# Routing of a fused attention and mixture-of-experts kernel: four chunks of tokens in place of two

## The chip, the cores and the metric

The kernel runs on one core of a Trainium2 chip. What counts is the device time of one execution in microseconds. Five engines work side by side, each through its own queue in order: TensorE (PE; PEld is its weight load), VectorE (DVE), ScalarE (ACT), GpSimd (POOL) and SyncE (SP), which issues most DMAs. Waits between engines are semaphores.

## The reference

Three layers follow each other: attention through 32 packed queries, a mixture of eight experts of which each token takes two, and a feed-forward layer. Cut to what matters here:

```python
p_packed = sm_attn(p, k, v)              # 4 batches, 8 heads, 576 rows, 64 wide
out = sm_attn(q, p_packed, p_packed)     # -> x: 2304 tokens x 512

logits = x @ w_gate                      # 8 experts
noisy_logits = logits + np.log1p(np.exp(x @ w_noise)) * noise
top2 = np.argpartition(-noisy_logits, 2, axis=1)[:, :2]
top2_w = softmax of the two chosen logits
for e in range(E):                       # h: 1024 wide
    out[mask] += top2_w * (np.maximum(x[mask] @ w1[e], 0.0) @ w2[e])

h = x @ w_in                             # 2048 wide
return (h * sigmoid(h)) @ w_out
```

## The kernel before

The 2304 tokens are 18 tiles of 128. Attention works them off in units of two tiles (tiles 8 and 17 alone). Its last phase, `unpacked` (L409), leaves for each tile a row block in DRAM (`xs`, L467) and 16 logits (`lg`, L462 and L464). A loop over 16 slots (L616) writes the attention phases of several units in turn; `START1`, `START2` and the `LAG`s say which phase stands in which slot.

`route` (L470) takes a chunk of n tiles and makes of its logits the row numbers by which tokens are fetched for the experts. It is a generator of eight to ten steps, nearly all on VectorE, each over all n tiles at once:

- noisy logits (rt_w, rt_sa, rt_h, rt_sp, rt_ny; L478 to L493; two steps on ScalarE),
- the two best experts of each token (L497, L499: one instruction a tile; rt_oh, rt_ob),
- a token's rank within its expert: matmuls into `rk` (L510 to L514) that count earlier tokens, those of earlier chunks through `seen_b`,
- rank into slot: rt_rs, rt_sf, rt_hi, rt_hs, rt_lo; then two one-hot tiles, rt_oc (L527, L529) and rt_oa (L534, three tiles a piece), whose product `ip` (L541, 2n matmuls) adds this chunk's tokens to the table of row numbers `idx_f`,
- slots and gates, by which the results are put together again much later (L567 to L581).

Before, there are two chunks. The first, tiles 0 to 10 (`EARLY` = 11), starts when their logits are there. From it comes `idx0`, the first 256 row numbers of expert 0 (L544), with which two gathers on GpSimd (`fetch`, L196) bring the rows of expert 0's first block. Tiles 11 to 17 are the second chunk; it is written within expert 0's first block (L661 to L672), beside its matmuls. When it is done (`idx`, L554), five more gathers bring three tiles for expert 0's second block and two for expert 1, which are transposed on TensorE (`transposed`, L153) and split into a high and a low part by ScalarE and VectorE.

`expert_block` (L235) runs eight steps f: twelve matmuls into `hps` (L208 to L210), relu and split on ScalarE (hh) and VectorE (hl, L232), and one step later the matmuls into `acc` (L218 to L220). The first block of expert 0 has 256 tokens, its second 384.

Up to the end of that first block a scheduler sets the order of each engine's queue by its own estimate of the times; the order in which the code is written is its input. Behind it, `pin` keeps TensorE and ScalarE in written order. The buffers of `rk`, `xp`, `pp`, `ip`, `c` and `i4` are two that go round (pool `pMx`).

Of the kernel before, what the change touches and what calls it, by code (L numbers as in the profile page):

```python
# [7 lines left out]
F32 = mybir.dt.float32  # L8
# [6 lines left out]
OP = mybir.AluOpType  # L15
AX = mybir.AxisListType
# [3 lines left out]
P = 128  # L20
B, H, S, D, PK = 4, 8, 576, 64, 32
N, DM, E, F, FF = 2304, 512, 8, 1024, 2048
NT = N // P
ET = 5
CAP = ET * P
# [5 lines left out]
START2 = (3, 4, 5, 5, 6, 6, 8, 11, 12, 12)  # L31
SWITCH = 12
WLOAD = 4
RSTEP = 3
LAG2 = (0, 1, 3, 3)
# [9 lines left out]
def body(ctx: ExitStack, tc: tile.TileContext, q, k, v, p, wg, wn, noise, w1, w2, w_in, w_out, out):  # L45
# [212 lines left out]
    with ExitStack() as ax:  # L258
# [211 lines left out]
        def route(t0, n, lg):  # L470

            def tl(shape, nm, dt=F32):
                return rt.tile([P, n, *shape], dt, name=f"rt_{nm}{n}", tag=f"rt_{nm}", bufs=1)
# [39 lines left out]
            for j in range(n - 1):  # L513
                T.matmul(rk[:, j + 1:, :], ones, ob[:, j:j + 1, :].to_broadcast([P, n - 1 - j, E]),  # L514
                         start=False, stop=j == n - 2)
            rs = tl([E], "rs")
# [25 lines left out]
            if t0 + n < NT:  # L542
                V.tensor_tensor(idx_f, idx_f, ip, op=OP.add)
                V.tensor_scalar(idx0, idx_f[:, 0:TA], 0.0, float((t0 + n) * P - 1), op0=OP.max, op1=OP.min)  # L544
                sn = rt.tile([P, E], F32, name=f"sn{n}")
                V.tensor_reduce(sn, ob.rearrange("p n e -> p e n"), axis=AX.X, op=OP.add)
                V.tensor_tensor(seen, seen, sn, op=OP.add)
                V.tensor_copy(seen_b, seen)
                c = pMx.tile([P, E], F32, name="c", tag="m")
                T.matmul(c, ones, seen_b, start=True, stop=True)  # L550
                V.tensor_scalar(few, c, float(TA * P), float(N), op0=OP.is_lt, op1=OP.mult)
            else:
                V.tensor_tensor(idx_f, idx_f, ip, op=OP.add)
                V.tensor_scalar(idx, idx_f, 0.0, float(N - 1), op0=OP.max, op1=OP.min)  # L554
                V.tensor_scalar(idx_f, idx_f, 0.0, float(N - 1), op0=OP.max, op1=OP.min)  # L555
                i4 = pMx.tile([P, 4, E * ET], F32, name="i4", tag="m")
                for g in range(4):
                    for a in range(4):
                        T.matmul(i4[32 * a:32 * a + 32, g, :], ident[:, 32 * g:32 * g + 32], idx_f, start=True, stop=True,
                                 tile_position=(0, 32 * a))  # L560
                V.tensor_scalar(idx4, i4, 4.0, quad[:, 0:1], op0=OP.mult, op1=OP.add)
                sn = rt.tile([P, E], F32, name=f"sn{n}")
                V.tensor_reduce(sn, ob.rearrange("p n e -> p e n"), axis=AX.X, op=OP.add)
                V.tensor_tensor(seen_b, seen, sn, op=OP.add)
# [4 lines left out]
            V.scalar_tensor_tensor(rr, ch, -float(CAP), sf, op0=OP.mult, op1=OP.add)  # L569
            V.tensor_scalar(late, rr, split_at - 63.5, None, op0=OP.is_ge)  # L570
            V.tensor_scalar(up, ch, float((TB - TA) * P), float((E - 1) * TA * P), op0=OP.mult, op1=OP.add)
# [5 lines left out]
            V.tensor_tensor(ex, m8[:, :, 1:2], m8[:, :, 0:1], op=OP.subtract)  # L577
# [6 lines left out]
        chunks = {0: EARLY, EARLY: NT - EARLY}  # L584
# [24 lines left out]
        def run(gen, n):  # L609
            for _ in range(n):  # L610
                next(gen, None)

        r0 = route(0, EARLY, lgs[0])
        W[0] = []
        M["delay"] = 2
        for slot in range(START2[-1] + LAG2[-1] + 1):  # L616
# [30 lines left out]
            if slot >= START2[5] + LAG2[3]:  # L647
                run(r0, RSTEP)
        for _ in r0:
            pass  # L650
        tick()
        tick()
        r1 = route(EARLY, NT - EARLY, lgs[EARLY])
# [7 lines left out]
        for f in expert_block(0, 0, TA, X["a"]):  # L661
            run(r1, 2)
            if f == 4:
                for _ in r1:
                    pass
# [290 lines left out]
```

## Time and profile before

| | us |
|---|---|
| time, median of 3 runs | 995.01 (994.36 to 996.98) |
| the profiled execution | 991.13 |
| its span in the profile | 989.30 |
| TensorE busy | 957.0 (97%) |
| VectorE busy | 447.4 (45%) |
| ScalarE busy | 346.4 (35%) |
| GpSimd busy | 313.4 (32%) |

The profile is one execution; 1.83 us of it lie outside the span. Attention and routing fill the first 118 us, expert 0's first block runs to 149 us, the other experts and the last layer fill the rest. The 97% of TensorE is a mean over stretches with different limits: a kernel of this kind is read by stretch.

### The profile page before, as it was taken

Reading aid. Unit: us, or ns where it says so; the run is one execution under the profiler, and the core shown is the slowest. Engines: PE = TensorE matmul, PEld = TensorE weight load, DVE = VectorE, ACT = ScalarE, POOL = GpSimd, SP = SyncE. Lnnn points to the kernel's source line nnn. Section 1 sums busy time; section 2 is a strip of 40 time slices with the busy share of each in tenths; the row PEclk is TensorE's granted clock in tenths of the full one; section 3 lists DMA queues with packets and bytes.
Section 4 is the critical chain, followed back from the end, with each engine's and each line's share of the span. In section 5 each row is a group of like instructions: output and inputs, shape, how many; then the busy total and the mean of one; then the engine's idle time right before and its main releaser. Section 6 shows DMA issues by size and latency. Waiting matters only on the chain.

```text
span 989.3 us, 14385 instructions
## 1 busy us (share of the span) xinstructions
PE 957.0 (97%) x5584; PEld 821.0 (83%) x5584; DVE 447.4 (45%) x871; ACT 346.4 (35%) x631; POOL 313.4 (32%) x345
## 2 busy tenths in 40 slices
PE   6989799999999999999999999999999999999996
PEld 4767589899999999998999988888888888888884
DVE  4537763666767576766634557222122221111111
ACT  3567322433434343433323343322222222222221
POOL 2166214343525243443200136333323322222221
PEclk9989899999999999999999999999999999999998
DMA  9994324576757676566623454111011110001001
GB/s 243 249 270 161 107 65 125 188 231 202 231 167 227 188 235 199 189 226 207 188 64 117 149 194 136 54 28 37 22 53 33 32 43 1 1 1 43 0 1 46
DMA packets 82298, 122.49 MB, mean 124 GB/s; under 512 B 16432, under 2 KB 49200, under 8 KB 82224
## 3 DMA queue, kind: packets, MB, share of 16 engines
q1 hardware_dynamic: 74704, 101.58, 32.6%
q0 software_dynamic: 7520, 19.93, 7.0%
q8 instruction: 46, 0.75, 0.3%
q14 instruction: 28, 0.23, 0.1%
HBM read 93.17 MB, written 28.31 MB: 123 GB/s over the span
## 4 chain that ended last, share of the span: by engine, by line
PE 90%; DVE 4%; DMA 3%; ACT 1%; SPq 1%; issue 1%; ACTq 0%
PE hps L208 14%; PE hps L210 14%; PE hps L209 14%; PE acc L219 14%; PE acc L218 14%; PE acc L220 14%; PE xp L460 1%; PE tps L157 1%; PE s L429 1%; PE s L362 1%; DMA vm<-in_v_dram 1%; DMA km<-in_k_dram 1%; DVE rt_oa L534 1%; PE kp L351 0%; DMA raw<-wf_out 0%
## 5 line engine op out<-in xcount | busy, mean ns | idle before, releaser
L176 POOL DMA_INDIRECT xg<-xs,idx x120 | 127.0, 1059 | 195.1 <-DVE xturn L185 147.6
L750 POOL TENSOR_TENSOR gl<-sg,gh 128x512 fp32r<-128x512 f32 (+1 forms) x80 | 95.4, 1194 | 253.5 <-ACT gh L749 237.9
L231 ACT ACTIVATE hh<-hps 128x384 fp32r<-128x384 f32 (+1 forms) x128 | 56.0, 438 | 260.5 <-PE hps L210 256.8
L746 DVE TENSOR_TENSOR sg<-hps,sg 128x512 f32<-128x512 f32 (+1 forms) x80 | 50.7, 634 | 196.2 <-ACT sg L745 196.0
L232 DVE SCALAR_TENSOR_TENSOR hl<-hps,hh 128x384 fp32r<-128x384 f32 (+1 forms) x128 | 62.4, 488 | 122.0 <-ACT hh L231 121.3
L745 ACT ACTIVATE sg<-hps 128x512 f32<-128x512 f32 (+1 forms) x80 | 44.2, 553 | 189.5 <-PE hps L210 189.2
L749 ACT ACTIVATE gh<-sg 128x512 fp32r<-128x512 f32 (+1 forms) x80 | 47.1, 589 | 79.3 <-DVE sg L746 79.1
L736 POOL DMA_INDIRECT y<-ys,slots x36 | 36.7, 1019 | 110.9 <-DVE hl L232 72.4
L739 DVE TENSOR_SCALAR y<-y,gates 128x512 f32<-128x512 f32 x18 | 10.9, 607 | 37.9 <-DMA y<-ys,slots 37.9
L740 DVE SCALAR_TENSOR_TENSOR y<-y,gates,y 128x512 f32<-128x512 f32 x18 | 15.7, 871 | 25.1 <-DMA y<-ys,slots 25.0
L460 PE MATMUL xp<-ppBD,a2T 128*128 128x272 f32 (+1 forms) x80 | 23.5, 433 | 1.6 <-ACT xr L51 0.8
L185 DVE STREAM_TRANSPOSE xturn<-xg 128x512 f32<-128x512 f32 x30 | 21.2, 706 | 3.7 <-DMA wf_in<-t 2.5
L689 DVE SCALAR_TENSOR_TENSOR t<-raw,t 128x512 int32<-128x512 int32 x32 | 22.2, 693 | 0.9
L690 DVE SCALAR_TENSOR_TENSOR t<-raw,t 128x512 int32<-128x512 int32 x32 | 22.1, 691 | 0.9
L196 POOL DMA_INDIRECT xg<-xs,idx x10 | 9.7, 969 | 40.3 <-DVE idx_f L555 19.5
L686 ACT ACTIVATE t<-raw 128x512 f32<-128x512 f32 x32 | 21.2, 662 | 0.1
L208 PE MATMUL hps<-xha,wa3h 128*128 128x256 f32 (+1 forms) x56 | 17.7, 316 | 1.8 <-DVE sg L746 1.8
L160 DVE TENSOR_TENSOR xla<-tps,xha 128x512 fp32r<-128x512 f32 x14 | 9.6, 690 | 21.1 <-ACT xha L159 21.1
L53 DVE COPY ysb<-acc 128x512 f32<-128x512 f32 x24 | 16.4, 682 | 4.9 <-PE acc L220 4.8
L429 PE MATMUL s<-ppT,qT 128*128 128x64 f32 x128 | 17.9, 291 | 0.0
L208 PE MATMUL hps<-xha,wa0h 128*128 128x256 f32 (+1 forms) x56 | 17.6, 314 | 0.2 <-ACT xha L159 0.2
L208 PE MATMUL hps<-xha,wa2h 128*128 128x256 f32 (+1 forms) x56 | 17.7, 316 | 0.1
(450 smaller groups left out, 2976.4 us busy)
## 6 DMA issues: line engine op xcount, KB each, us to landing
raw<-in_moe_w_dram SPq DMA_DIRECT2D x56, 512.0 KB, 4.0
ys<-ysb SPq DMA_DIRECT2D x40, 256.0 KB, 3.7
raw<-in_moe_w_in_dram SPq DMA_DIRECT2D x16, 512.0 KB, 4.3
raw<-in_moe_w_out_dram SPq DMA_DIRECT2D x16, 512.0 KB, 4.1
xs<-xr SPq DMA_DIRECT2D x18, 256.0 KB, 2.1
km<-in_k_dram SPq DMA_DIRECT2D x8, 512.0 KB, 7.6
vm<-in_v_dram SPq DMA_DIRECT2D x8, 512.0 KB, 7.6
qm<-in_q_dram SPq DMA_DIRECT2D x8, 512.0 KB, 7.1
```

The source lines that it names most:

```text
L176: G.indirect_dma_start(out=xg[:, g * P:(g + 1) * P], out_offset=None, in_=xs[:, :].rearrange("n (a f) -> (n a) f", a=4), in_offset=bass.In ...
L208: T.matmul(ps, wh[:, c, s], xh[:, c, :n], start=c == 0, stop=False)
L209: T.matmul(ps, wh[:, c, s], xl[:, c, :n], start=False, stop=False)
L210: T.matmul(ps, wl[:, c, s], xh[:, c, :n], start=False, stop=c == 3)
L218: T.matmul(y, hh[:, s], wh[:, f % 2, :], start=f == 0, stop=False)
L219: T.matmul(y, hh[:, s], wl[:, f % 2, :], start=False, stop=False)
L220: T.matmul(y, hl[:, s], wh[:, f % 2, :], start=False, stop=f == last)
L231: A.activation(hh, ps, AF.Relu)
L232: V.scalar_tensor_tensor(hl, ps, 0.0, hh.bitcast(F32), op0=OP.max, op1=OP.subtract)
L746: V.tensor_tensor(sg, ps, sg, op=OP.mult)
L749: A.activation(gh, sg, AF.Copy)
L750: G.tensor_tensor(gl, sg, gh.bitcast(F32), op=OP.subtract)
```

## The change

`route` is called for four chunks, of tiles 0 to 5, 6 to 10, 11 to 14 and 15 to 17. A table, `ROUTE`, says in which slot how many steps of which chunk are written; the steps of the last chunk that are left are written in the first step f of expert 0's block. The routing tiles have two buffers (`bufs=2`) in place of one. The count `seen` is brought up right behind the rank matmuls, `idx0` and `few` are made only after tile 10, and three instructions that begin slots and gates are kept in written order behind the row numbers (`keep_in_program_order`).

```diff
-RSTEP = 3
+ROUTE = {8: ((0, 4),), 9: ((0, 99), (6, 3)), 10: ((6, 99),), 14: ((11, 5),), 15: ((11, 99), (15, 3))}
...
-                return rt.tile([P, n, *shape], dt, name=f"rt_{nm}{n}", tag=f"rt_{nm}", bufs=1)
+                return rt.tile([P, n, *shape], dt, name=f"rt_{nm}{n}", tag=f"rt_{nm}", bufs=2)
...
+            sn = rt.tile([P, E], F32, name=f"sn{t0}", tag="rt_sn", bufs=2)
+            V.tensor_reduce(sn, ob.rearrange("p n e -> p e n"), axis=AX.X, op=OP.add)
+            V.tensor_tensor(seen, seen, sn, op=OP.add)
+            V.tensor_copy(seen_b, seen)
             rs = tl([E], "rs")
...
-                V.tensor_scalar(idx0, idx_f[:, 0:TA], 0.0, float((t0 + n) * P - 1), op0=OP.max, op1=OP.min)
...
+                if t0 + n == EARLY:
+                    V.tensor_scalar(idx0, idx_f[:, 0:TA], 0.0, float((t0 + n) * P - 1), op0=OP.max, op1=OP.min)
+                if t0 + n == EARLY:
+                    c = pMx.tile([P, E], F32, name="c", tag="m")
...
-            V.scalar_tensor_tensor(rr, ch, -float(CAP), sf, op0=OP.mult, op1=OP.add)
+            tc.keep_in_program_order(V.scalar_tensor_tensor(rr, ch, -float(CAP), sf, op0=OP.mult, op1=OP.add))
...
-        chunks = {0: EARLY, EARLY: NT - EARLY}
+        chunks = {0: 6, 6: 5, 11: 4, 15: 3}
...
-            if slot >= START2[5] + LAG2[3]:
-                run(r0, RSTEP)
-        for _ in r0:
-            pass
+            for t, k in ROUTE.get(slot, ()):
+                run(rs[t], k)
...
         for f in expert_block(0, 0, TA, X["a"]):
-            run(r1, 2)
+            run(rs[15], 99)
             if f == 4:
-                for _ in r1:
-                    pass
                 rows = fetch(xs[:, :], idx, TA, TB) + fetch(xs[:, :], idx, ET, TA)
```

How this moves instructions shows at two places. The first is VectorE's queue where attention is at its seventh unit; sd, mx, kT and s are attention's tiles, lg the logits. Before:

```order
L368 TENSOR_REDUCE mx<-s_1139 128x1
L462 TENSOR_TENSOR lg_201<-xp,lg_201 128x16
L369 TENSOR_SCALAR mx<-mx 128x1
L443 TENSOR_REDUCE mx_1046<-sd_1048 128x16
L444 TENSOR_SCALAR mx_1046<-mx_1046 128x16
L445 RECIPROCAL mx_1046<-mx_1046 128x16
```

After:

```order
L369 TENSOR_SCALAR mx<-mx 128x1
L478 TENSOR_TENSOR rt_w_1205<-lg_201 128x48
L479 TENSOR_SCALAR rt_sa_1208<-lg_201 128x48
L483 TENSOR_SCALAR rt_sp_1207<-lg_201 128x48
L482 TENSOR_SCALAR rt_h_1206<-rt_w_1205 128x48
L485 TENSOR_SCALAR rt_big_1209<-rt_w_1205 128x48
L484 TENSOR_TENSOR rt_h_1206<-rt_h_1206,rt_w_1205 128x48
L443 TENSOR_REDUCE mx_1048<-sd_1050 128x16
L487 SCALAR_TENSOR_TENSOR rt_h_1206<-rt_h_1206,rt_w_1205 128x48
L444 TENSOR_SCALAR mx_1048<-mx_1048 128x16
L487 SCALAR_TENSOR_TENSOR rt_h_1206<-rt_h_1206,rt_w_1205 128x48
L445 RECIPROCAL mx_1048<-mx_1048 128x16
```

The first steps of the chunk of six now stand ahead of and between attention's steps, some 12 us earlier in the program than the first steps of the chunk of eleven did.

The second place is TensorE's queue at the end of expert 0's first block (numbers of lines that the change has shifted are those of the changed file). Before, the transposes of the five gathered tiles (tps, four instructions a tile) stand apart: two times 8 ahead of the acc matmuls of f = 5 and f = 6, and the last 4 here, ahead of those of f = 7:

```order
L220 MATMUL acc<-wa7h,hl 128x512 x2
L157 MATMUL tps<-ident,xg 128x128 x4
L218 MATMUL acc<-wa7h,hh 128x512
L219 MATMUL acc<-wa7l,hh 128x512
L218 MATMUL acc<-wa7h,hh 128x512
L219 MATMUL acc<-wa7l,hh 128x512
L220 MATMUL acc<-wa7h,hl 128x512 x2
L208 MATMUL hps<-xhb,wa0h 128x384
```

After (i is idx4's matmul, c the count):

```order
L220 MATMUL acc<-wa7h,hl 128x512 x2
L561 MATMUL i_2027<-idx_f,ident 32x40 x16
L662 LDWEIGHTS ones
L662 MATMUL c<-seen_b,ones 128x8
L218 MATMUL acc<-wa7h,hh 128x512
L219 MATMUL acc<-wa7l,hh 128x512
L218 MATMUL acc<-wa7h,hh 128x512
L219 MATMUL acc<-wa7l,hh 128x512
L220 MATMUL acc<-wa7h,hl 128x512 x2
L157 MATMUL tps<-ident,xg 128x128 x20
L208 MATMUL hps<-xhb,wa0h 128x384
```

All five tiles are now transposed in a row ahead of the second block's first matmul (hps of xhb), and the matmuls of the last ip, which before stood ahead of the fifth of the eight steps f, stand ahead of the hps of the last one; those of i, before behind the fifth hps, stand behind the last.

## Rows read from the trace of the kernel before

**Rows 1.** Busy time by stretch: stretch, length, busy of each engine, PEclk, DMA.
```profile
120.00:150.00 30.00, 29.29 (x232) 24.28 (x231) 18.41 (x85) 8.38 (x21) 4.76 (x5) 1.00 0.22 70
150.00:300.00 150.00, 150.00 (x836) 136.44 (x836) 92.67 (x141) 56.36 (x93) 59.87 (x58) 1.00 0.62 194
```

**Rows 2.** Busy time by stretch, as rows 1: PE, PEld, DVE, ACT, POOL.
```profile
77.00:90.00 13.00, 12.64 (x106) 9.98 (x105) 7.92 (x31) 11.90 (x29) 4.71 (x6) 1.00 0.64 219
90.00:110.00 20.00, 13.23 (x199) 10.43 (x198) 19.63 (x92) 7.17 (x21) 8.71 (x17) 0.89 0.29 94
110.00:118.50 8.50, 7.33 (x42) 4.72 (x39) 4.98 (x14) 4.20 (x11) 3.77 (x4) 0.85 0.40 125
```

**Rows 3.** Timeline of VectorE, tiles 0 to 10: start, duration, instruction.
```profile
89.82 0.25 DVE L478 TENSOR_TENSOR rt_w<-lg 128x88 f32<-128x88 f32 x1
...
109.70 0.17 DVE L544 TENSOR_SCALAR idx<-idx_f 128x2 int32<-128x2 f32 x1
```

**Rows 4.** Timeline of VectorE, tiles 11 to 17.
```profile
122.52 0.22 DVE L478 TENSOR_TENSOR rt_w<-lg 128x56 f32<-128x56 f32 x1
...
128.37 0.41 DVE L232 SCALAR_TENSOR_TENSOR hl<-hps,hh 128x256 fp32r<-128x256 f32 x1
...
134.34 0.18 DVE L554 TENSOR_SCALAR idx<-idx_f 128x40 int32<-128x40 f32 x1
```

**Rows 5.** Timeline of GpSimd's weight splits and of VectorE beside and apart from them.
```profile
76.87 2.78 POOL L119 TENSOR_TENSOR wa5l<-raw,wa5h 128x256 fp32r<-128x256 f32 x4
...
91.14 2.86 POOL L119 TENSOR_TENSOR wa6l<-raw,wa6h 128x256 fp32r<-128x256 f32 x4 [5.03 <-PE pp L388]
91.96 0.77 DVE L487 SCALAR_TENSOR_TENSOR rt_h<-rt_h,rt_w 128x88 f32<-128x88 f32 x1
...
95.14 2.81 POOL L119 TENSOR_TENSOR wa7l<-raw,wa7h 128x256 fp32r<-128x256 f32 x4
97.19 0.17 DVE L577 TENSOR_TENSOR rt_ex<-rt_m 128x11 f32<-128x11 f32 x1
...
123.36 0.22 DVE L487 SCALAR_TENSOR_TENSOR rt_h<-rt_h,rt_w 128x56 f32<-128x56 f32 x1
```

**Rows 6.** Timeline around the gathers (in brackets idle before), and how long they take to land.
```profile
110.79 1.15 POOL L196 DMA_INDIRECT xg<-xs,idx  x1 [6.32 <-PE s L436]
...
133.51 0.55 PE L541 MATMUL ip<-rt_oc,rt_oa 128*128 128x40 f16 x8 [0.55 <-DVE rt_oa L534]
134.79 0.98 POOL L196 DMA_INDIRECT xg<-xs,idx  x1 [19.45 <-DVE idx_f L555]
139.82 0.95 POOL L196 DMA_INDIRECT xg<-xs,idx  x1 [0.30 <-issue]
DMA to landing us min/median/max: 3.5/3.6/3.7
```

**Rows 7.** Timeline of TensorE at the end of expert 0's first block.
```profile
136.26 0.49 PE L559 MATMUL i<-idx_f,ident 128*32 128x40 f32 x32
...
136.72 0.47 PE L218 MATMUL acc<-wa6h,hh 128*128 128x512 f32 x1
...
145.11 0.28 PE L208 MATMUL hps<-xha,wa3h 128*128 128x256 f32 x1
...
147.01 0.60 PE L157 MATMUL tps<-ident,xg 128*128 128x128 f32 x4
...
149.02 0.45 PE L208 MATMUL hps<-xhb,wa0h 128*128 128x384 f32 x1
```

**Rows 8.** TensorE by stretch (length, busy, granted clock, DMA), and one wait.
```profile
54.00:56.00 2.00, 2.00 (x13) 0.64 1.03 322
60.00:62.00 2.00, 2.00 (x46) 0.65 1.09 305
104.00:106.00 2.00, 0.65 (x4) 0.94 0.21 68
104.53 0.65 PE L451 MATMUL a2p<-ident,sd 128*128 128x128 f32 x4 [1.94 <-POOL sd L446]
```

More of the change, by code (lines that the diff above doesn't have):

```diff
@@ L543, in route @@
                 V.tensor_tensor(idx_f, idx_f, ip, op=OP.add)
-                V.tensor_scalar(idx0, idx_f[:, 0:TA], 0.0, float((t0 + n) * P - 1), op0=OP.max, op1=OP.min)
[L545 to L551, printed above, removed]
+                if t0 + n == EARLY:
+                    V.tensor_scalar(idx0, idx_f[:, 0:TA], 0.0, float((t0 + n) * P - 1), op0=OP.max, op1=OP.min)
+                if t0 + n == EARLY:
+                    c = pMx.tile([P, E], F32, name="c", tag="m")
+                    T.matmul(c, ones, seen_b, start=True, stop=True)
+                    V.tensor_scalar(few, c, float(TA * P), float(N), op0=OP.is_lt, op1=OP.mult)
             else:
@@ L561, in route @@
                 V.tensor_scalar(idx4, i4, 4.0, quad[:, 0:1], op0=OP.mult, op1=OP.add)
-                sn = rt.tile([P, E], F32, name=f"sn{n}")
-                V.tensor_reduce(sn, ob.rearrange("p n e -> p e n"), axis=AX.X, op=OP.add)
-                V.tensor_tensor(seen_b, seen, sn, op=OP.add)
             yield
@@ L568, in route @@
             rr, late, up = tl([2], "rr"), tl([2], "late"), tl([2], "up")
-            V.scalar_tensor_tensor(rr, ch, -float(CAP), sf, op0=OP.mult, op1=OP.add)
+            tc.keep_in_program_order(V.scalar_tensor_tensor(rr, ch, -float(CAP), sf, op0=OP.mult, op1=OP.add))
             V.tensor_scalar(late, rr, split_at - 63.5, None, op0=OP.is_ge)
-            V.tensor_scalar(up, ch, float((TB - TA) * P), float((E - 1) * TA * P), op0=OP.mult, op1=OP.add)
+            tc.keep_in_program_order(V.tensor_scalar(up, ch, float((TB - TA) * P), float((E - 1) * TA * P), op0=OP.mult, op1=OP.add))
             V.tensor_tensor(up, up, late, op=OP.mult)
@@ L576, in route @@
             ex, dn = tl([1], "ex"), tl([1], "dn")
-            V.tensor_tensor(ex, m8[:, :, 1:2], m8[:, :, 0:1], op=OP.subtract)
+            tc.keep_in_program_order(V.tensor_tensor(ex, m8[:, :, 1:2], m8[:, :, 0:1], op=OP.subtract))
             A.activation(ex, ex, AF.Exp)
@@ L611, in run @@
                 next(gen, None)
-        r0 = route(0, EARLY, lgs[0])
+        rs = {t: route(t, n, lgs[t]) for t, n in chunks.items()}
         W[0] = []
@@ L646, in body @@
                         load_w2(W[0], 0, i - 4, G)
-            if slot >= START2[5] + LAG2[3]:
-                run(r0, RSTEP)
-        for _ in r0:
-            pass
+            for t, k in ROUTE.get(slot, ()):
+                run(rs[t], k)
         tick()
         tick()
-        r1 = route(EARLY, NT - EARLY, lgs[EARLY])
         for i in "ab":
```

## The prediction

> **What bounds the kernel now.** I read the busy time by stretch first, then TensorE's waits, then VectorE's instructions in order of time in the stretch where TensorE is not full. From 120 us on TensorE is busy nearly without a gap: 29.29 of 30 us, then 150.00 of 150 [rows 1]. So whatever the change does to the moment when the long expert stage begins is passed on whole to the end, and whatever it does to VectorE after that is hidden. What is left to win lies ahead: between 90 and 118.5 us TensorE is busy 20.56 of 28.5 us, 7.9 us idle, while VectorE is busy 19.63 of the first 20 [rows 2]. That is the routing of tiles 0 to 10, from 89.82 us (rt_w) to 109.70 (idx, the first row numbers) [rows 3], with attention's steps for the last tiles queued among it. Between 77 and 90 us it is the other way round: TensorE is busy 12.64 of 13 us, VectorE 7.92, so VectorE has 5.1 us idle there [rows 2].
>
> The second half, tiles 11 to 17, runs on VectorE from 122.52 to 134.52 us [rows 4], beside the first block of expert 0 on TensorE. Its row numbers feed five gathers on GpSimd; their rows must lie in SBUF, transposed, when the second block (hps at 149.02) begins [rows 6, 7]. Today that has much room.
>
> **The change, term 1: the gathers behind the last chunk.** In the order of the changed kernel the last row numbers come far later relative to expert 0's first block. Before, ip of the second half stands ahead of the fifth of the block's eight steps f. Now three tiles have a chunk of their own, whose ip stands just ahead of the last hps (f = 7), and all five transposes, 20 instructions, stand between the block's last matmul and the second block's first. From the end of ip to that hps two things race.
> - The gathers: ip ends at 133.51 + 0.55 = 134.06; idx ends at 134.34 + 0.18 = 134.52, so 0.46; the first gather starts 0.27 later, at 134.79; the fifth at 139.82, so 5.03 more; a gather lands 3.6 us after it starts (3.5 to 3.7) [rows 4, 6]; the last transpose takes 0.44 (four matmuls at the 0.11 pitch of full clock, estimated from the row of four at 147.01, 0.60 long with the pipeline's tail, next start after 0.35 to 0.44) [rows 7]. Sum 0.46 + 0.27 + 5.03 + 3.6 + 0.44 = 9.8 us.
> - TensorE's own work: from the first hps of f = 7 to the second block's hps before, 145.11 to 149.02, 3.9 us with one transposed tile in it; four more tiles at 0.44, 1.8; the matmuls of idx4 and c, 0.46 (136.26 to 136.72) [rows 7]. Sum 6.1 us.
>
> So TensorE idles 9.8 - 6.1 = **3.7 us**, where before it idled nothing (the rows were there). This supposes that VectorE is in time for ip. Laying its steps for tiles 15 to 17 against TensorE's steps f = 4 to 6, I find oa done about 1 us ahead of ip, so the term is 3.6 to 3.8 if that holds, and up to 5.2 if VectorE is 1.5 us later than I think.
>
> **Term 2: the clock behind that stall.** TensorE's granted clock is at 1.2 GHz, half of full, in two stretches. In the first it falls inside 54 to 56 us (mean 0.64) and rises inside 60 to 62 (0.65): 1.4 + 4 + 1.4 = 6.8 us. The second begins just ahead of 106 us (0.94 over 104 to 106), after TensorE had been busy 0.65 us of 2, and had idled 1.94 us ahead of that [rows 8]; 102.6 us, where this idling began, is 3.2 us earlier. The new stall is of that kind: five transposes, 2.2 us of work, in some 6 us. If the clock falls 3.2 us into it and stays down for 6.8, then 6.8 - (5.9 - 3.2) = 4.1 us of dense matmuls run at half speed and cost 2.0 more. No row shows a stall that is 37% busy, so the ends are 0 (it stays up) and 3.4 (it falls as the stall ends: half of 6.8). I take **2.0**.
>
> **Term 3: VectorE from 77 to 110 us.** A chunk has a cost that doesn't depend on its tiles. Eleven tiles take 89.82 to 109.87, 20.05 us; in this lie 14 attention instructions, 4.1 us from start to start, and 2.4 us of slowed instructions (below), so 13.6 us pure [rows 3]. Seven tiles take 122.52 to 134.41, 11.9 us; less three hl steps (0.41 a piece, 0.35 from start to start) and 0.4 of idling, 10.4 us pure [rows 4]. The difference, 3.2 us for four tiles, gives 0.8 us a tile and 4.9 fixed. Two chunks of 6 and 5 instead of one of 11 add 4.9 us of VectorE ahead of idx. (The other two add as much beside expert 0, where VectorE has room and only term 1 feels it.) Slots and gates behind the row numbers move some 10 small instructions behind idx only for the chunk of 5; those of the chunk of 6 still run ahead of it. The few tiny matmuls more are inside TensorE's idle time.
>
> Against this the chunk of 6 starts at about 77 us, in VectorE's 5.1 us of idle time. VectorE's order is fixed, and routing steps now stand ahead of attention steps that TensorE waits for (the reduction of sd, kT, px), so not all of it is won: I take 4.1.
>
> Some of the steps run slower beside GpSimd. While GpSimd splits weights (from 91.14 us, four pieces of 0.7) L487, 0.22 alone, takes 0.77, one per piece [rows 5]; by such rows the slowed steps of the chunk of 11 cost those 2.4 us. The chunk of 6 begins right in the split of wa5l, 76.87 to 79.65 [rows 5], and the chunk of 5 has its first steps beside the wa6l split, as the 11 had. So the slowing grows by 0 to 2.5 us (the rest of that split); I take 1.5, since most of the chunk's first steps are small. It could also vanish (-2.4).
>
> The tail behind idx gets shorter: before, the first gather starts at 110.79, 0.92 behind idx, since a matmul of the last attention tile ended late; 0.27 is enough [rows 4, 6]. And the 0.55 us wait for oa ahead of ip at 133.51 has no partner now. Together -1.1 (0.65 and 0.45).
>
> Sum of term 3: 4.9 + 1.5 - 4.1 - 1.1 = **+1.2**. Ends: 4.9 - 2.4 - 5.1 - 1.1 = -3.7; 4.9 + 2.5 - 3.1 - 1.1 = +3.2.
>
> A row speaks on the slowing: L577, with two inputs in SBUF but 11 elements, takes 0.17 us at 97.19, beside the split of wa7l (95.14 to 97.95), and is not slowed [rows 5]. The Trainium skill (GPSIMD Engine Reference, Specifications) says that GpSimd's SBUF interfaces are shared with VectorE, with contention for instructions that have two SBUF inputs or run in a 2-port mode, without a size below which it doesn't matter. By the row tiny steps are free and term 3 is as above; by the rule all of them wait, which is the last rival below.
>
> **The sum.** 3.7 + 2.0 + 1.2 = +6.9 us. The profiled execution, 991.13 us (its span 989.30 and 1.83 around it), would become 998.0; the median of the runs shown is 995.01, 3.9 above the profiled one, and the same difference gives **1001.9 us**.
>
> **The rivals.**
> - *The slack takes it all, no change.* The chunk of 6 fits into the 5.1 us and nothing is slowed: -3.7, against the 3.7 of the gathers, clock 0 to 2: 995 to 997, say 996. For it speaks the idle time [rows 2]; against it that VectorE's queue is in order.
> - *Faster.* Routing in small pieces lets TensorE fill the holes between 90 and 118.5 us: all 7.9 us go, and the late stall keeps its clock: -7.9 + 3.7 = -4.2, 990.8 us. It decides when idx is ready by about 103 us, 6.9 earlier than 109.87. Against it: VectorE is busy 27.6 of the 33 us from 77 to 110 [rows 2], and gets 4.9 more.
> - *All small steps wait for GpSimd.* Each chunk's steps queue behind pieces of 0.7 and 1.05 us: term 3 about +5.3, VectorE late for ip as well, term 1 5.2, term 2 3.4: +13.9, 1009.
> - That the change doesn't do what it says is part of my forecast: it asks for the last chunk earlier (by f = 0), yet its end stands later in the order.
>
> **Chances.** Forecast 0.57, +3 to +12 us; no change 0.22; faster 0.12; all slowed 0.09. A difference under 0.3% (3.0 us) can't be told from none here. Faster by more 0.12, within 0.22, slower 0.57 + 0.09 = 0.66. The terms' ends give 3.6 + 0 - 3.7 = -0.1 to 5.2 + 3.4 + 3.2 = +11.8; to leave out no more than 0.2 the range goes to 1007 above and to 992 below, into the faster case.
>
> **What would show it.** Term 1: TensorE's transposes tps after the last acc of expert 0's first block, each waiting for a gather about 1.26 us apart, some 3.7 us of idling in the 6 us ahead of the first 384-wide hps, with the first gather within 0.5 us behind ip's end. Term 2: a granted clock near 0.5 behind it. Term 3: idx of tiles 0 to 10 at about 112 us, not 109.7; VectorE without idle time from 77 us on; rt_h steps of 0.7 us around 78 us. I am wrong if the fifth gather lands before the block's last matmul, if idx is ready before 106 us, or if TensorE runs out of rows but keeps its clock and the first expert starts 4 us sooner.

## The result and the profile after

The changed kernel takes 1007.8 us against 995.3 us, both medians of six runs: 1.33% more, with a 95% interval of 1.16 to 1.51%, or about 12.5 us. The forecast was 6.9 us slower, 1001.9, with a range to 1007. The sign held; the size did not. (A later comparison of the same two kernels gave 1.40%, 1.16 to 1.64.)

The profiled execution has a span of 1004.9 us, 15.6 more than before. TensorE by stretch, in the columns of [rows 1, 2]:

```profile
77.00:90.00 13.00, 11.49 (x98) 8.29 (x97) 12.57 (x59) 11.26 (x26) 6.57 (x9) 1.00 0.58 192
90.00:110.00 20.00, 15.29 (x188) 12.55 (x186) 17.97 (x83) 8.05 (x22) 7.36 (x16) 0.78 0.32 100
110.00:118.50 8.50, 7.99 (x45) 5.54 (x44) 7.90 (x30) 2.86 (x7) 4.45 (x4) 0.51 0.11 32
150.00:300.00 150.00, 144.51 (x821) 130.24 (x821) 88.68 (x147) 55.12 (x92) 57.65 (x56) 0.98 0.59 183
```

VectorE is now busy 12.57 of 13 us between 77 and 90, where it had 7.92 [rows 2]: the chunk of 6 did fill that idle time. TensorE, however, is at half speed for longer ahead of the first expert (granted clock 0.78 and 0.51 where it was 0.89 and 0.85), and behind 150 us, where before it was busy 150.00 of 150 [rows 1], it loses 5.5 us. How long it is at half speed there varies: 17.1 us in both profiles of the changed kernel, 6.8 and 13.7 in the two of the kernel before (the second pair is used below). The place of the loss behind 150 us is the end of expert 0's first block. Timeline of TensorE there (start, duration, instruction; in brackets how long it idled and for whom), the counterpart of [rows 7]:

```profile
148.75 0.32 PE L545 MATMUL ip<-rt_oc,rt_oa 128*128 128x40 f16 x6
...
152.47 0.62 PE L220 MATMUL acc<-wa7h,hl 128*128 128x512 f32 x2
153.05 0.66 PE L157 MATMUL tps<-ident,xg 128*128 128x128 f32 x4
154.53 0.66 PE L157 MATMUL tps<-ident,xg 128*128 128x128 f32 x4 [0.82 <-DMA xg<-xs,idx]
156.47 0.63 PE L157 MATMUL tps<-ident,xg 128*128 128x128 f32 x4 [1.29 <-DMA xg<-xs,idx]
158.60 0.63 PE L157 MATMUL tps<-ident,xg 128*128 128x128 f32 x4 [1.50 <-DVE xlb L160]
159.69 1.09 PE L157 MATMUL tps<-ident,xg 128*128 128x128 f32 x4 [0.47 <-DMA xg<-xs,idx]
162.19 0.69 PE L208 MATMUL hps<-xhb,wa0h 128*128 128x384 f32 x1 [1.41 <-DVE xla L160]
162.68 0.52 PE L209 MATMUL hps<-xlb,wa0h 128*128 128x384 f32 x1
...
166.14 0.34 PE L208 MATMUL hps<-xhb,wa0h 128*128 128x384 f32 x1
```

The five waits in brackets sum to 5.49 us: four ahead of a gathered tile, and 1.41 for the split of the last one. The third is put down to VectorE's xlb, but it is most likely the gather's as well: the transposes write two buffers in turn, and in the second profile of this kernel the same wait, 2.14 us, is the gather's. The clock falls among the waits: the last four transposes take 1.09 us in place of some 0.6, and twelve 384-wide matmuls from 162.19 on start 0.32 apart instead of 0.175, 1.75 us more. The second block's first hps stands at 162.19; before, it stood at 149.02 [rows 7]. So 13.2 of the span's 15.6 us lie ahead of this point, and 1.75 right behind it.

Of the 13.2 us, 1.8 are put down to chance. The profile is late by that much at 68 us, where the queues of both kernels still hold the same instructions in the same order (the first difference comes behind 77 us); a second pair of profiles (below) has 0.7 there.

### The profile page after: what moved, and what is told of

Read it like the earlier page. It is cut to its first block, busy times and chain, and to the rows that moved or that the text cites. A ratio compares the mean times of both kernels' runs of the same rounds, so it can differ in the third digit from the quotient of the medians.

```text
span 1004.9 us, 14472 instructions
## 1 busy us (share of the span) xinstructions
PE 964.3 (96%) x5588; PEld 827.0 (82%) x5588; DVE 458.2 (46%) x952; ACT 348.5 (35%) x637; POOL 315.6 (31%) x345
## 2 busy tenths in 40 slices
DMA packets 82301, 122.52 MB, mean 122 GB/s; under 512 B 16432, under 2 KB 49200, under 8 KB 82224
## 4 chain that ended last, share of the span: by engine, by line
PE 87%; DMA 4%; DVE 3%; SPq 2%; ACT 1%; POOL 1%; issue 1%; ACTq 0%; POOLq 0%; DVEq 0%
PE hps L208 14%; PE hps L210 14%; PE hps L209 14%; PE acc L218 14%; PE acc L219 13%; PE acc L220 13%; PE xp L460 1%; PE tps L157 1%; DMA vm<-in_v_dram 1%; DMA xs<-xr 1%; PE s L429 1%; DMA km<-in_k_dram 1%; DMA y<-ys,slots 1%; PE qp L422 1%; PE s L362 0%
## 5 line engine op out<-in xcount | busy, mean ns | idle before, releaser
L429 PE MATMUL s<-ppT,qT 128*128 128x64 f32 x128 | 21.1, 324 | 1.6 <-DVE rt_oh L522 1.6
L429 PEld LDWEIGHTS s<-ppT,qT 128*128 128x128 f32 x128 | 20.1, 240 | 2.0 <-issue 1.7
L208 PE MATMUL hps<-xhb,wa0h 128*128 128x384 f32 (+1 forms) x48 | 17.9, 373 | 1.4 <-DVE xla L160 1.4
L351 PE MATMUL kp<-ident,km 128*128 128x128 f32 x64 | 10.5, 297 | 8.6 <-DMA km<-in_k_dram 8.2
```

What stands on the lines that cost most here:

```text
L208: T.matmul(ps, wh[:, c, s], xh[:, c, :n], start=c == 0, stop=False)
L429: T.matmul(s2[:, :, h, :], qT[:, h, :], ppT[b, h // 4][:, h % 4], start=True, stop=True)
```

## Experiments

The ratios stand against runs of the kernel before in the same comparison, in brackets their 95% intervals; a ratio of 1.0010 is about 1 us. The comparisons differed: in some the kernel before takes 995, in others 1004 us, so ratios are compared, and profiles only within one comparison where a few microseconds matter.

### Which half costs what

Three kernels put the changed kernel together piece by piece. The routing's buffers are one per half in them, not two as in the changed kernel; the third of them, which has this and the order alone, shows that it costs nothing.

```diff
# second half whole
-chunks = {0: 6, 6: 5, 11: 4, 15: 3}
+chunks = {0: 6, 6: 5, 11: 7}        # routed inside expert 0's first block, as before
# first half whole
+chunks = {0: 11, 11: 4, 15: 3}      # the late two written in slots 14 and 15, as changed
# order only
+chunks = {0: 11, 11: 7}             # with slots and gates pinned behind the row numbers
```

> Chunks of 6, 5 and 7: the first half stays split, the second half is one chunk again. Theory A (most of the +12.5 us is the late row numbers of the last chunk, 1.3% of 995; the split of the first half costs only what it adds to the first gathers, 3.3 us in the two profiles once 1.8 us that the changed kernel's run lost in its first loads are taken off): TensorE no longer idles ahead of the second block, and the time is 3 to 4.5 us above the kernel before (998 to 999.5). Theory B (the split of the first half pushes all of VectorE's later work back, so the last row numbers are late with one chunk as well): 8 us or more above before, and TensorE still waits for gathers at the end of the first block.

> Chunks of 11, 4 and 3: the first half is one chunk, the second half stays split. Theory A: the first gathers start as in the kernel before (near 111 us), the wait for the last gathers stays but shorter, since the last ip now stands about one step f earlier (3 us): 2 to 3 us of idle time in place of 5.5, 1 to 2 for the lower clock behind it, in all 3 to 6 us above before (998 to 1001). Theory B (the first half's split is the source of all): within 1.5 us of the kernel before.

> Chunks of 11 and 7 as before, with the change's other edits alone (slots and gates pinned behind the row numbers, the counts moved ahead). Theory A: no cost, -1 to +1 us against the kernel before. Theory C (the pinned slots and gates hold VectorE up where the last row numbers are due): 2 us or more above before.

Measured: second half whole 1.0056 (1.0040 to 1.0072), first half whole 1.0062 (1.0040 to 1.0083), order only 0.9997 (0.9982 to 1.0011). The order of slots and gates costs nothing: theory C falls. The halves cost about the same, 5.6 and 6.2 us, and add up to 11.8 of the change's 12.5 to 13.9. Theory A had given the first half 3 to 4.5, so it was too small there, and theory B falls, since either half alone costs something. With the first half whole TensorE waits 2.07 us ahead of the second block, 1.41 of it for the last tile's split, as theory A said; with the second half whole it waits there for the split alone (1.46).

### Does the block wait for five gathers?

```diff
-                rows = fetch(xs[:, :], idx, TA, TB) + fetch(xs[:, :], idx, ET, TA)
+                rows = fetch(xs[:, :], idx, TA, TB)
...
+            box["a"] = fetch(xs[:, :], idx, ET, TA)    # expert 1's rows: behind the second block's start
```

> The changed kernel, with the two gathers and transposes for expert 1 moved behind the start of expert 0's second block, so that this block waits for three gathers and not five. Theory A (the gathers come 1.26 us apart, and the second block waits for the fifth): 2 x 1.26 = 2.5 us less idle time ahead of the second block and 2 transposed tiles moved out of the half-speed stretch; 3 to 4 us under the changed kernel, so 8.5 to 9.5 above before (about 1004). Rival D (the wait is set by the first gather and by the clock, not by the number of gathers): within 1.5 us of the changed kernel (1006 to 1009).

Measured: 1.0088 (1.0066 to 1.0111), 4.5 to 5.2 us under the changed kernel's ratios of 1.0133 and 1.0140. Timeline of TensorE in this kernel:

```profile
154.42 0.66 PE L157 MATMUL tps<-ident,xg 128*128 128x128 f32 x4 [0.19 <-DMA xg<-xs,idx]
155.91 0.65 PE L157 MATMUL tps<-ident,xg 128*128 128x128 f32 x4 [0.83 <-DMA xg<-xs,idx]
157.72 1.12 PE L157 MATMUL tps<-ident,xg 128*128 128x128 f32 x4 [1.15 <-DVE xlb L160]
160.25 0.69 PE L208 MATMUL hps<-xhb,wa0h 128*128 128x384 f32 x1 [1.41 <-DVE xlb L160]
```

Two gathers fewer, and 3.58 us of waits instead of 5.49. The clock still falls (1.12 us for the third tile). Rival D falls and theory A holds (its 8.5 to 9.5 us above before are met, the saving against the changed kernel is a little larger than its 3 to 4): the block is held up by the number of gathers behind the row numbers.

### Why the row numbers are late

The program writes the routing of the two late chunks in slots 14 and 15, ahead of the last attention units, where before it wrote the second half inside expert 0's first block. Two kernels write them there again, one with the first half split, one with it whole.

```diff
-ROUTE = {8: ((0, 4),), 9: ((0, 99), (6, 3)), 10: ((6, 99),), 14: ((11, 5),), 15: ((11, 99), (15, 3))}
+ROUTE = {8: ((0, 4),), 9: ((0, 99), (6, 3)), 10: ((6, 99),)}
...
         for f in expert_block(0, 0, TA, X["a"]):
-            run(rs[15], 99)
+            if f < 4:
+                run(rs[11 if f < 2 else 15], 99 if f % 2 else 3)
```

> The kernel before, unchanged, for a profile on the same chip as the others. Every theory: ratio 1 within 0.2%.

> The changed kernel, unchanged, for a profile on the same chip as the others. Every theory: 1.1 to 1.5% above the kernel before (the first comparison gave 1.33%). If the 1.8 us by which the first profile was late before any instruction stands in another order is chance, it shows in this pair of profiles no more, or with another size; if it is the change's, it shows again.

> All four chunks, but the program writes the routing of tiles 11 to 14 and 15 to 17 behind the last attention tiles (between steps f = 0 and f = 3 of expert 0's first block), where the second half was written before, and not in slots 14 and 15. In the order this brings the last ip from step f = 7 to f = 5.5, with three of the five transposed tiles inside the block. Theory A2 (the late row numbers come from where the two late chunks are written: their steps go ahead of the last tiles' attention and push its last xp from 122 to 138 us, so the number of chunks as such does not cost there): the wait for gathers is gone, and the time is that of the kernel with only the first half split, 5 to 6.5 us above before. Rival E (a chunk's fixed cost on VectorE is what makes the last row numbers late, wherever it is written): 8 us or more above before, with TensorE still waiting for gathers.

> Chunks of 11, 4 and 3, with the two late ones written between steps f = 0 and f = 3 of expert 0's first block, as in the run before that had all four chunks. Theory A2 (the late chunks cost by where they are written, not by being two): -0.5 to +1.5 us against the kernel before. Rival E (a fixed cost per chunk shows there too): 3 us or more above.

Measured: the kernel before 1.0007 (0.9993 to 1.0021), the changed kernel 1.0140 (1.0116 to 1.0164), four chunks with the late ones written in the block 1.0044 (1.0027 to 1.0061), and the late split alone, so written, 0.9994 (0.9977 to 1.0011). Timelines of the four-chunk kernel, TensorE and then GpSimd:

```profile
143.01 0.32 PE L545 MATMUL ip<-rt_oc,rt_oa 128*128 128x40 f16 x6
148.71 1.03 PE L157 MATMUL tps<-ident,xg 128*128 128x128 f32 x8
152.41 1.03 PE L157 MATMUL tps<-ident,xg 128*128 128x128 f32 x8
154.67 0.60 PE L157 MATMUL tps<-ident,xg 128*128 128x128 f32 x4
156.73 0.45 PE L208 MATMUL hps<-xhb,wa0h 128*128 128x384 f32 x1 [1.46 <-DVE xla L160]
...
144.06 0.98 POOL L196 DMA_INDIRECT xg<-xs,idx  x1 [23.68 <-DVE idx_f L557]
149.09 0.95 POOL L196 DMA_INDIRECT xg<-xs,idx  x1 [0.30 <-issue]
```

The last ip stands at 143.01 us instead of 148.75, four of the five tiles are transposed inside the block, and no gather is waited for (the split of the last tile still is, 1.46 us). So 13.9 - 4.4 = 9.5 us of the change come from where the late chunks are written, not from their being two: rival E falls, and with the first half whole nothing that can be measured is left (0.9994). What the writing order does is seen in the attention: in the changed kernel the last xp, from which the logits of tile 17 come, starts at 137.9 us, 14.3 behind expert 0's first hps; before, it started at 121.9, 3.4 behind it. In the four-chunk kernel it starts 7.7 behind it (131.9), so the split of the first half alone also pushes attention into the block. The chunk of 3 has its first step (rt_w) at 138.84 us, right behind these logits; the chunk of 7 had it at 122.52 [rows 4].

The two profiles of the same comparison also show what of the first profile was chance. First TensorE's last `s` of a unit ahead of any difference in order, then VectorE's first row numbers, first of the kernel before, then of the changed one:

```profile
67.74 0.69 PE L436 MATMUL s<-ppT,qT 128*64 128x64 f32 x16
111.39 0.17 DVE L544 TENSOR_SCALAR idx<-idx_f 128x2 int32<-128x2 f32 x1
```

```profile
68.42 0.69 PE L436 MATMUL s<-ppT,qT 128*64 128x64 f32 x16
114.50 0.15 DVE L549 TENSOR_SCALAR idx<-idx_f 128x2 int32<-128x2 f32 x1
```

From the one to the other it is 43.65 and 46.08 us: the first row numbers come 2.4 us later by the change. (In the first pair it was 43.4 and 46.1.)

### The clock in the stall

```diff
         for c in range(4):
             pin(T.transpose(ps[:, c, :], src(c), ident))
+        if again:                       # 8 for the first four of the five tiles
+            fill = pMx.tile([P, 4, P], F32, name="fill", tag="m")
+            for c in range(again):
+                T.transpose(fill[:, c % 4, :], src(c % 4), ident)
```

> The changed kernel with eight more transposes of the same tile (0.9 us, the result unused) behind each of the first four of the five transposed tiles, so that TensorE works while it waits for the gathers. Theory A: the clock keeps 2.4 GHz, or falls later; of the half-speed stretch (about 1.75 us over twelve 384-wide hps, and 1 more on the last transposes) 1.5 to 2.5 us come back: that much under the changed kernel. Rival F (the clock falls whatever TensorE does there, or the added work stands in the way): no gain, or up to 2 us more.

Measured: 1.0112 (1.0090 to 1.0134), 2.8 us under the changed kernel in the same comparison, a bit more than expected; the two intervals overlap, so the size is rough. TensorE by stretch, first in the changed kernel of that comparison, then with the added transposes:

```profile
150.00:160.00 10.00, 5.66 (x64) 3.95 (x62) 5.14 (x21) 2.86 (x6) 4.76 (x5) 0.98 0.60 181
160.00:170.00 10.00, 8.53 (x36) 7.72 (x37) 2.07 (x4) 2.18 (x4) 5.55 (x6) 0.68 0.35 97
```

```profile
150.00:160.00 10.00, 8.86 (x95) 7.36 (x94) 5.29 (x22) 2.87 (x6) 4.76 (x5) 1.00 0.61 184
160.00:170.00 10.00, 8.43 (x51) 7.93 (x50) 2.40 (x4) 2.07 (x4) 6.11 (x7) 1.00 0.33 96
```

Busy 8.86 instead of 5.66 us of ten, TensorE keeps its 2.4 GHz; the wait for the gathers stays. Rival F falls. In the two traces the way from ip to the first hps is 0.8 us shorter with the added transposes (13.37 against 14.20), and the nine matmuls behind it take 1.70 us instead of 2.97: 2.1 us by this count. With the 2.8 us of the run times, 9.5 - 2.8 = 6.7 are the stall itself.

### What the split of the first half costs

The first attempt put a copy by ScalarE in the place of GpSimd's split of wa5 to wa7.

```diff
+        if eng is A:
+            A.activation(lo, src, AF.Copy)
+            return
...
-                        load_w2(W[0], 0, i - 4, G)
+                        load_w2(W[0], 0, i - 4, G if i < 5 else A)
```

> The changed kernel without GpSimd's split of the weights wa5 to wa7 of expert 0: their low parts are a copy that ScalarE makes (so the low parts hold other values; the work left out is twelve GpSimd pieces of 0.7 us). Theory G (GpSimd's pieces slow VectorE's routing steps, one step of 0.1 to 0.2 us becoming 0.5 to 0.8 per piece, by the trace some 3.5 to 5 us of VectorE between 78 and 105 us): the first row numbers come 2 to 4 us sooner and the time is 2 to 4 us under the changed kernel (ratio to before 1.010 to 1.012). Rival H (those steps are not on the path to the row numbers, TensorE or ScalarE is): within 1.5 us of the changed kernel.

> The kernel before with the same work left out. Theory G: before loses by the same slowing the 2.4 us of VectorE that its trace shows; 1 to 2.5 us under the kernel before (ratio 0.9975 to 0.999), so the slowing grows with the change by the difference of the two, 1 to 2 us. Rival H: within 1 us of before, and the same saving in both kernels would say that the slowing did not grow.

Measured: 1.0094 (1.0072 to 1.0116) for the changed kernel, 1.0049 (1.0033 to 1.0066) for the one before. Without the splits the kernel before gets slower, which neither theory has: ScalarE's three copies probably were work that it had no room for (the first rt_w starts 26.3 us behind the `s` row above, 23.5 before). As a measure of the slowing the pair is of no use. Its one clean number is from the changed kernel's trace: first row numbers 43.2 us behind that `s` row, 2.9 sooner than with the splits.

The second attempt takes the splits away and puts nothing in their place; the third leaves the computation whole and moves them behind the first two gathers, where GpSimd has nothing to do.

```diff
# without low parts (wa5 to wa7)
-                    W[0].append(weight_tile(wa, "wa", i))
+                    hi, lo = weight_tile(wa, "wa", i)
+                    W[0].append((hi, lo if i < 5 else hi))      # and split() returns where lo is hi
# splits behind
-                if slot == s0 + WLOAD:
+                if slot == (s0 + WLOAD if i < 5 else 7 + i):    # and GpSimd's pieces pinned there
```

> The kernel before without the low parts of expert 0's weights wa5 to wa7: no GpSimd split, nothing in its place (the high part is read where the low part was, so those products hold other values). Theory G (GpSimd's pieces cost the chunk of 11 the 2.4 us of slowed steps that the trace shows): the first row numbers about 2 us sooner, 1 to 2.5 us under before. Rival H: within 1 us of before.

> The same work left out of the kernel with four chunks whose late two are written behind the last attention tiles (that kernel was 4.4 us above before). Theory G1 (its cost is mostly the slowing beside GpSimd): within 1.5 us of the same kernel without splits and one first chunk (so 1 to 2.5 under before or up to 0.5 above). Theory G2 (fixed cost of a second chunk on VectorE, some 2 us and more, and the slowing grows by 2.4 to 5 only): 2 to 4 us above the kernel of one first chunk without splits.

> The kernel before, whole computation, with the three splits of wa5 to wa7 on GpSimd behind the first two gathers (their loads three slots later), where GpSimd idles until 134 us. Theory G: 1 to 2.5 us under before, if the splits are done by step f = 2 of expert 0's first block. Rival M (the splits then slow the second half's routing, or TensorE waits for wa5l): the same as before or up to 3 us above.

> The four chunks with the late two written behind the last attention tiles, and the three splits behind the first two gathers. Theory G1: about the kernel before with the splits moved the same way, and so under the kernel before. Theory G2: 2 to 4 us above that one, 0 to 3 above before.

Measured, against the kernel before: without the splits, chunks as before 1.0022 (1.0008 to 1.0035), four chunks with the late ones in the block 0.9996 (0.9984 to 1.0008); with the splits behind, as before 1.0011 (0.9998 to 1.0024), four chunks 1.0019 (1.0007 to 1.0031).

So the four chunks cost 4.4 us with the splits in their old place, 1.9 with the splits moved and nothing (-0.4) without them. Theory G2, the fixed cost of a second chunk, falls by the pair without splits: four chunks are 2.6 us under one first chunk there, where it had them 2 to 4 above. The chunk of 6 is hidden in VectorE's idle time, and without the splits the row numbers come at 109.22 us, 42.1 behind the `s` row, sooner than before the change. The pair with the splits moved (0.8 us apart) does not decide between the theories. Of G1 the slowing holds, as the rows below show; its numbers were not all met, since the kernels with one first chunk gain nothing without the splits (+2.2 us) or with them moved (+1.1). With the splits gone or moved the scheduler also writes attention's steps in another order, in all four kernels. In the two with one first chunk rt_w then starts 1 to 3 us later. From rt_w to the last FIND_INDEX8 the chunk of 11 does get shorter, 7.4 to 5.7 us, but from there to idx it gets longer, 12.5 to 13.8. So the 4.8 us between 1.0044 and 0.9996 are not exact.

The rows show the slowing itself. GpSimd and VectorE in the changed kernel, chunk of 5:

```profile
97.45 2.78 POOL L119 TENSOR_TENSOR wa6l<-raw,wa6h 128x256 fp32r<-128x256 f32 x4 [7.51 <-PE pp L388]
101.39 2.77 POOL L119 TENSOR_TENSOR wa7l<-raw,wa7h 128x256 fp32r<-128x256 f32 x4
...
97.00 0.20 DVE L478 TENSOR_TENSOR rt_w<-lg 128x40 f32<-128x40 f32 x1
97.53 0.70 DVE L484 TENSOR_TENSOR rt_h<-rt_h,rt_w 128x40 f32<-128x40 f32 x1
98.84 0.76 DVE L489 TENSOR_TENSOR rt_sa<-rt_sa,lg 128x40 f32<-128x40 f32 x1
99.63 0.63 DVE L568 SCALAR_TENSOR_TENSOR rt_rr<-chosen,rt_sf 128x12 f32<-128x12 f32 x1
101.44 0.73 DVE L492 TENSOR_TENSOR rt_ny<-rt_sp,nzt 128x40 f32<-128x40 f32 x1
102.77 0.73 DVE L578 TENSOR_SCALAR rt_dn<-rt_ex 128x6 f32<-128x6 f32 x1
103.41 0.22 DVE L497 MAX8 rt_m<-rt_ny 128x8 f32<-128x8 f32 x2
104.58 0.15 DVE L499 FIND_INDEX8 rt_i<-rt_m,rt_ny 128x8 uint32<-128x8 f32 x1
```

The same steps in the four-chunk kernel without the splits:

```profile
95.35 0.20 DVE L480 TENSOR_TENSOR rt_w<-lg 128x40 f32<-128x40 f32 x1
96.37 0.20 DVE L491 TENSOR_TENSOR rt_sa<-rt_sa,lg 128x40 f32<-128x40 f32 x1
96.59 0.17 DVE L570 SCALAR_TENSOR_TENSOR rt_rr<-chosen,rt_sf 128x12 f32<-128x12 f32 x1
97.82 0.20 DVE L494 TENSOR_TENSOR rt_ny<-rt_sp,nzt 128x40 f32<-128x40 f32 x1
98.30 0.17 DVE L580 TENSOR_SCALAR rt_dn<-rt_ex 128x6 f32<-128x6 f32 x1
99.53 0.16 DVE L501 FIND_INDEX8 rt_i<-rt_m,rt_ny 128x8 uint32<-128x8 f32 x1
109.22 0.16 DVE L551 TENSOR_SCALAR idx<-idx_f 128x2 int32<-128x2 f32 x1
```

A step of 6 elements takes 0.73 us instead of 0.17. From rt_w to idx the chunk of 5 needs 17.2 us beside the splits (97.00 to 114.19) and 13.9 without (95.35 to 109.22): 3.3 us for eight pieces. The kernel that leaves the computation whole and only moves the splits has the same 13.9:

```profile
98.10 0.20 DVE L480 TENSOR_TENSOR rt_w<-lg 128x40 f32<-128x40 f32 x1
102.28 0.16 DVE L501 FIND_INDEX8 rt_i<-rt_m,rt_ny 128x8 uint32<-128x8 f32 x1
111.97 0.16 DVE L551 TENSOR_SCALAR idx<-idx_f 128x2 int32<-128x2 f32 x1
```

All of the difference lies in the steps beside the splits, which stand in the same order in the three kernels: from rt_w to the end of the last FIND_INDEX8 it is 7.73 us against 4.34 and 4.34, from there to idx 9.46 against 9.53 and 9.53. For this chunk attention's new order and the half-speed stretch (17.1 us in the changed kernel, 6.8 and 10.2 in the other two) make no difference.

### An attempt to beat both

```diff
+        ins = A.activation(hi, src, AF.Copy)
+        if eng is G and hi is W[0][0][0]:
+            tc.keep_in_program_order(ins)
+        else:
+            pin(ins)
```

> The kernel before, with one instruction put later on ScalarE: the copy of expert 0's first weight (wa0h, at 51.98 us, waiting 3.29 us for its load) no longer stands ahead of attention's a1T, for which TensorE waits 2.93 us and behind which its clock is at half for 6.8 us. Theory K (that wait and the clock behind it are on TensorE's path, since TensorE is full from 54 to 90 us): 3 to 6 us under before. Rival L (the loads bound that stage, or VectorE's routing takes the gain up): within 1.5 us of before.

Measured: 1.0070 (1.0049 to 1.0090), slower. TensorE does keep its clock to 58 us, but then idles from 58 to 61 for the next step, its clock falls there instead (0.50 from 62 to 64), and the `s` row comes at 66.72, no sooner than in the first profile of before (66.31); the first row numbers come 47.7 us behind it. Theory K falls, and more is lost than rival L has; what exactly was not followed up. (From 104 to 120 us the granted clock is 0.50 there, 0.79 and 0.60 in the two profiles of the kernel before; whether that is the cause was not tried.) None of these kernels beats the one before; the nearest that keeps the computation whole is the late split alone, at 0.9994.

## Why the prediction was right and wrong

The direction and the three mechanisms were right; two of the three terms were too small. Term 1 ended its chain at the last transposes and left out the split that follows, and took the landing of a gather from a quieter moment. Term 3 took one row to say that tiny steps are not slowed, and counted a gain behind idx that came in no run.

| step of the prediction | said | measured |
|---|---|---|
| term 1, gathers behind the last chunk | +3.7 (3.6 to 5.2) | +6.7 (9.5 less the clock); 6.9 in the first profile |
| term 2, the clock behind that stall | +2.0 (0 to 3.4) | +2.8; 2.1 in the traces |
| term 3, VectorE to the first row numbers | +1.2 (-3.7 to +3.2) | +4.4 (the split of the first half in all) |
| sum | +6.9 | +13.9 in that comparison, +12.5 in the first |

**What bounds the kernel** was right: all that delays the long expert stage came out at the end, and slots and gates were worth nothing.

**Term 1** had the right mechanism, the place (the transposes behind the last acc) and the pitch (1.28 and then 1.25 us), but its chain was cut off too early. By its own steps in the first profile: ip ends at 148.75 + 0.32 = 149.07; the first gather starts at 149.80, 0.73 later as predicted; the fifth at 154.83, 5.03 later as predicted; its tile is transposed from 159.69 on, 4.86 behind its start where the landing was put at 3.6; and the first hps comes 2.50 behind that, where the sum had 0.44. In these 2.50 lie the transposes at half clock (1.09) and the split of the last tile by ScalarE and VectorE, for which TensorE waits 1.41. The sum left that split out, though the second block's first matmuls wait for it. 13.1 us in all against 9.8; TensorE's own work was 6.2 with the clock at full, near the 6.1 predicted. So the stall was 6.9 us by this profile, and the chain 3.3 longer than said: 1.3 for the landing, 1.4 for the split, 0.6 for the last transposes at half clock.

The landing has a cause that the sum could not take from the rows before. Right behind the block's last matmul the stores of its results (ys, two of 256 KB) are issued, at 153.79 us, and the last gathers move beside them; of the gathers whose landing the profile shows, two took 4.7 and 4.9 us. In the four-chunk kernel above the stores are issued at 155.53, when the gathers have landed, and these took 3.3 to 3.8. No run moved the stores alone, so this is read from the times.

The first and the last of the five gathers, the stores, and the time to landing, then that of the four-chunk kernel:

```profile
149.80 0.98 POOL L196 DMA_INDIRECT xg<-xs,idx  x1 [29.99 <-DVE idx_f L557]
154.83 0.95 POOL L196 DMA_INDIRECT xg<-xs,idx  x1 [0.30 <-issue]
153.79 0.81 SPq L249 DMA_DIRECT2D ys<-ysb  x2
DMA to landing us min/median/max: 3.2/4.7/4.9
...
DMA to landing us min/median/max: 3.3/3.5/3.8
```

**Term 2** was of the right size, and the reason (TensorE little busy in the stall) is the one that the filled stall showed.

**Term 3** had the moment of the first row numbers nearly right, 2.4 us late in the second pair of traces where 4.9 + 1.5 - 4.1 = 2.3 was said, but by luck: its parts were off in opposite ways. The fixed cost of 4.9 us was real work but hidden: without the splits the two chunks are no later than the one. (The seven tiles of its estimate also end at 134.52, not 134.41 [rows 4], which makes some 0.3 us.) The slowing beside GpSimd costs more than was said: 3.4 us in the chunk of 5, and less in the chunk of 6. There rt_w, rt_sa, rt_sp and rt_h (0.44, 0.74, 0.77 and 0.77 at 79.0 to 80.7), among them the steps of 0.7 us that the prediction said would show, are some 2 us longer in all, but the chunk of 5's rt_w comes only 0.6 later behind the chunk of 6's than without the splits (18.0 against 17.4). The chunk of 11 had lost 1.7 us (7.4 against 5.7), so by this count the slowing grew by 2.3 to 3.7 us, where 1.5 was taken and 2.5 was the end. The -1.1 behind idx was wrong as well: 0.65 of it was to come from the first gather starting 0.27 behind idx instead of 0.92, and it starts 0.92 behind idx in every profile here, the changed kernel's too, so no late matmul had held it up. The step that failed in the slowing is the reading of one row: L577, 0.17 us at 97.19, was taken to say that tiny steps are not slowed [rows 5]. Read closer, the last GpSimd piece of that split starts in the same instant:

```profile
97.19 0.76 POOL L119 TENSOR_TENSOR wa7l<-raw,wa7h 128x256 fp32r<-128x256 f32 x1
```

L577 sat on the seam between two pieces and probably got in first; the piece took 0.76, the other three of that split 0.72. One row was no evidence for a size below which steps are free. The Trainium skill (SBUF — State Buffer, Who interferes with whom) says that a VectorE instruction with two inputs in SBUF contends with a GpSimd instruction that reads SBUF, that the same holds in a 2-port mode, and that whoever issues first holds the ports while the other waits for the whole instruction. The rows above agree: 0.63 to 0.76 us for steps of 0.17 to 0.20 alone, up to about one piece (0.70 from start to start) however small the step, and MAX8, with one input, beside the last piece is not slowed.

**The rivals.** "All small steps wait for GpSimd" had 1009 us, and its parts for terms 3 and 1 (5.3 and 5.2) were nearer to what was measured than the forecast's; for term 2 (3.4) the measurement does not tell. It was given 0.09. Its one wrong part is that VectorE would be late for ip: TensorE did not wait for oa there, so that its 5.2 came near 6.7 by luck. "The slack takes it all" was right on the fixed cost and wrong on the slowing. The predicted signs were seen: five transposes with gathers 1.25 us apart, idling ahead of the first hps (5.5 us where 3.7 were said), the clock at half behind it, rt_h of 0.77, idx at 112.4 in the changed kernel once the chance 1.8 us are taken off (predicted 112).

What stays open is how the 4.4 us of the first half divide. In the trace of that kernel they show as a first hps 3.3 us later behind the `s` row than before (57.4 against 54.0) and a first block 2.2 us longer (32.5 against 30.3, 1.46 of it the wait for the last tile's split), which no term of the prediction has. The slowed steps lie ahead of the first hps; what attention's new order and the half-speed stretch add there was not separated, since each kernel without the splits also moved attention's steps.

## What to carry to other kernels

A chain that ends a prediction goes to the instruction that waits, with every engine that touches the data on the way: here a gathered tile still had to be transposed, split by two engines and only then read, and TensorE's clock was at half when it went on. Where the code was written decided more here than how it was cut: the same four chunks cost 13.9 us written ahead of the last attention units and 4.4 behind them, so the place in the program is tried before the number of chunks. Small VectorE steps were not small beside GpSimd here; many cost up to one GpSimd piece (0.73 us for 0.17), and a single unslowed row proves nothing until the piece's own start is looked up.

## What the runs showed of the hardware

TensorE's low clock early in the program is not the same from run to run, though the instructions are the same and in the same order. In the stretch behind the idle time between 50 and 62 us it lasted 6.8 us in one profile of the kernel before [rows 8] and 3.4 in the other, and 10.2 in both of the changed kernel, with TensorE busy nearly all the time. The `s` row stands between 66.31 and 69.93 us in the profiles of this case. Single profiles of this kernel are therefore compared from a common point, not from zero.

The same kernel took 1004 us in two comparisons and 995 in the others. That is not tied to the number of the chip in the record: number 0 has 1004.5 in one comparison and 994.7 in a later one. The order-only kernel's waits, from one of the slower comparisons, show ScalarE 31.4 us in waits for nothing that the profile shows (engine, line, waited for; total, times, longest):

```profile
ACT hh L231 <- issue: 31.4, 16, 3.5
```

A line of this kind, of 24.6 to 34.9 us, is in all eight profiles of the two slower comparisons and in none of the others. The cause was not tried.
